# Two attentions in a row: an order of instructions planned by a list scheduler, queries in natural order, second scores over 128 rows, and a shared product for two tails

## The chip, the core and the metric

One NeuronCore of a Trainium2 chip runs the whole program. Its engines work side by side, each through its own instructions in order: TensorE (PE) multiplies matrices into PSUM, eight banks of 512 fp32 columns; VectorE (DVE) and ScalarE (ACT) read PSUM and write SBUF; GpSimd (POOL) works on SBUF alone; SyncE (SP) issues DMAs. Engines wait for each other by semaphores. The metric is the device time in microseconds.

## What is computed

For 8 batches and 8 heads of 576 positions and 64 columns, a first attention keeps only weights near the maximum; its heads side by side are the input x of a second, causal one with four experts, of which each position uses two. The reference in short, the sums and the gates' working left out:

```python
scores = scale * np.matmul(q, k.transpose(0, 1, 3, 2))
thresh = np.max(scores, axis=-1, keepdims=True) - tau
scores = np.where(scores >= thresh, scores, -1000000000.0)
attn = np.exp(scores - np.max(scores, axis=-1, keepdims=True))
x = (attn / sum) @ v                      # heads side by side: B, S, 512
...
for e in range(E):
    q, k, v = x @ wq[e], x @ wk[e], x @ wv[e]
    a = causal_softmax(scale * (q @ k.T))
    out += gate_e * (a @ v @ wo[e])       # gates: softmax of the 2 largest of x @ w_gate
```

## The kernel before

**Tiles.** A pair is two heads of one batch: 32 pairs. A pair has four score tiles of 128 queries by 576 keys for each head, and a fifth in which the 64 left-over queries of both heads stand as 128 rows, the *tail* (order of tiles: `TS = (4, 0, 1, 2, 3)`, 4 being the tail). fp32 operands are split into a rounded part (hi) and a rest (lo), and a product is hi·hi + hi·lo + lo·hi. DMAs spread k as `kt` and q as `qt` over 128 rows, so that two matmuls do for three terms (line 283). A loaded query tile holds every fourth position, since a partition takes four neighbouring rows of q at once; q and k are copied whole, and q scaled, before PE transposes them (`prep`, lines 256 to 310).

**First stage.** For a score tile: matmuls into one of two double banks `s`; VectorE takes the maximum (350) and the threshold `thr`, one instruction for each head (352); ACT the exponential (355); VectorE masks and sums (357); POOL normalizes (365); PE transposes `pp` (tm, tt), ACT or VectorE copies the results to `pt`, `ptt`; PE multiplies them by v in groups of tiles; the result is split into x.

**Second stage**, once for a batch, for two pairs of experts (`ep`): projections (pj), values (v) and gates; scores `s<-q,q` with 64-row operands, the two experts in the two halves of PE's rows, three terms each, then a mask; maximum, exponential, scaling on POOL; transposes (t), value products, and an output product of six 512-wide matmuls for each of five query tiles, the fifth of 64 rows. For the last batch the projections over two of the four pairs are made ahead and added later (`CUT`).

**Order.** PE's order is written out: each matmul follows the last by an explicit dependency, and a counter `pe[1]` adds up estimated PE time. Each of 160 first-stage steps has a share of 5.7 us; pieces of the second stage are put in when the counter passes a due time set at the piece before, transposes (T2) for instance so long after the scores:

```python
AFTER_S2, AFTER_V, AFTER_T2, AFTER_AV2 = 7000, 8500, 1800, 2000
...
        T2.append((pe[1] + AFTER_S2, b, t, ep))
```

The other engines are ordered by priorities (`PR`). The prediction names lines by the numbers of the listing.

Of the kernel before, what the change touches and what calls it, by code (L numbers as in the profile page):

```python
# [53 lines left out]
}  # L54
PPB = 4
P2B = 3
PTB = 9
PTTB = 4
VB = 3
E_PTT = "A"  # L60
# [3 lines left out]
def kernel(  # L64
# [13 lines left out]
    nc = tc.nc  # L78
    B, H, S, D = q.shape
    E = wq.shape[0]  # L80
    DM = H * D
    P = 128
    R = 4
    SM = R * P
    ST = S - SM
    HS = S // 2
    NPAIR = H // 2
    NC = DM // P
    EP = E // 2
    NV = E * D + E  # L90
    SCALE = 1.0 / math.sqrt(D)

    const = ctx.enter_context(tc.tile_pool(name="const", bufs=1))
    one = ctx.enter_context(tc.tile_pool(name="one", bufs=1))
    two = ctx.enter_context(tc.tile_pool(name="two", bufs=2))
    small = ctx.enter_context(tc.tile_pool(name="small", bufs=4))
    ps_s = ctx.enter_context(tc.tile_pool(name="ps_s", bufs=2, space=PSUM))
    ps_g = ctx.enter_context(tc.tile_pool(name="ps_g", bufs=4, space=PSUM))

    now = [0, 0]  # L100

    def pr(what):

        now[1] += 20
        tc.cur_priority = 20000000 + int((now[0] + PR.get(what, 0.0)) * 1000000) + now[1]

    def gbank(name, dt=F32):
        return ps_g.tile([P, 512], dt, tag="g", name=name)


    ident = const.tile([P, P], F32, name="ident")
    make_identity(nc, ident)
    ident_b = const.tile([P, P], BF16, name="ident_b")
    nc.gpsimd.tensor_scalar(ident_b, ident, 1.0, 0.0, op0=ALU.mult, op1=ALU.add)
    mask = const.tile([P, P], BF16, name="mask")
    nc.gpsimd.memset(mask, 0.0)
    nc.gpsimd.affine_select(out=mask, in_=mask, compare_op=ALU.is_ge, fill=NEG, base=0,
                            pattern=[[-1, P]], channel_multiplier=1)
    mask2 = const.tile([P, ST], BF16, name="mask2")
    nc.gpsimd.memset(mask2, 0.0)  # L120
    for j in range(2):
        nc.gpsimd.affine_select(out=mask2[j * ST:(j + 1) * ST], in_=mask2[j * ST:(j + 1) * ST],
                                compare_op=ALU.is_ge, fill=NEG, base=0,
                                pattern=[[-1, ST]], channel_multiplier=1)
    tie = const.tile([P, E, E], F32, name="tie")
    nc.gpsimd.memset(tie, 1.0)
    nc.gpsimd.affine_select(out=tie, in_=tie, compare_op=ALU.is_gt, fill=0.0, base=0,
                            pattern=[[1, E], [-1, E]], channel_multiplier=0)


    def rounded(dst, src, scale=1.0):
        nc.gpsimd.tensor_scalar(dst, src, scale, 0.0, op0=ALU.mult, op1=ALU.add)

    def rest(dst, src, hi):
        nc.gpsimd.tensor_tensor(dst, src, hi.bitcast(F32), op=ALU.subtract)

    def copy(e, dst, src):
        if e == "A":
            nc.scalar.activation(dst, src, AF.Copy)  # L139
        elif e == "D":  # L140
            nc.vector.tensor_copy(dst, src)
        elif e == "X":
            nc.any.tensor_copy(dst, src)  # L143
        else:
            rounded(dst, src)


    NOSYNC = mybir.DependencyInfo(mybir.DependencyClass.NoSync, mybir.DependencyReason.DATA)
    pe = [None, 0.0, None]

    def queued(r, x, ns):
        if pe[0] is not None:
            tc.add_manual_dep(r.ins, pe[0].name, NOSYNC, reason="order")
        shape = (x.shape[0], math.prod(x.shape[1:]))
        pe[0], pe[1], pe[2] = r.ins, pe[1] + ns + (190 if shape != pe[2] else 0), shape

    def matmul(out, x, y, **kw):
        w = math.prod(y.shape[1:])
        ns = 60 if x.dtype == BF16 else 0.81 * w if x.dtype == F32 else w / 2.4 + 11
        queued(nc.tensor.matmul(out, x, y, **kw), x, ns if x.shape[0] == P else ns / 2)  # L160

    def transpose(out, x):
        queued(nc.tensor.transpose(out, x, ident), x, 109)  # L163

    def minus(e, dst, a, b):
        (nc.vector if e == "D" else nc.gpsimd).tensor_tensor(dst, a, b, op=ALU.subtract)

    VS = {}  # L170
    qm = const.tile([P, 2, R + 1, D], F32, name="qm")
    km = const.tile([P, 2, R + 1, D], F32, name="km")
    for t in (qm, km):
        nc.vector.memset(t[ST:, :, R], 0.0)
    vtz = [const.tile([P, 2, D], F32, name=f"vtz{i}") for i in range(VB)]
    for t in vtz:
        nc.gpsimd.memset(t, 0.0)

    def load_pair(n):
        b, hp = divmod(n, NPAIR)  # L180
        hs = slice(2 * hp, 2 * hp + 2)
        vm = one.tile([P, 2, R, D], F32, tag="vm", name=f"vm_{n}", bufs=VB)
        pr("ld")
        def load(dst, src):
            r = nc.sync.dma_start(dst, src)
            if n in (1, 2):
                tc.add_manual_dep(r.ins, SPREAD[0].name, NOSYNC, reason="order")
        for t, x in ((km, k), (qm, q)):
            load(t[:, :, :R], x[b, hs, :SM, :].rearrange("h (p r) d -> p h r d", r=R))
            load(t[:ST, :, R], x[b, hs, SM:, :].rearrange("h s d -> s h d"))  # L190
        load(vm, v[b, hs, :SM, :].rearrange("h (p r) d -> p h r d", r=R))
        for j, rows in enumerate((slice(0, ST), slice(ST, P))):
            load(vtz[n % VB][rows, j], v[b, 2 * hp + j, SM:, :])
        VS[n] = (vm, vtz[n % VB])


    wqh = const.tile([P, NC, E * D], F32R, name="wqh")
    wql = const.tile([P, NC, E * D], F32R, name="wql")
    wkh = const.tile([P, NC, E * D], F32R, name="wkh")
    wkl = const.tile([P, NC, E * D], F32R, name="wkl")  # L200
    wvh = const.tile([P, NC, NV], F32R, name="wvh")
    wvl = const.tile([P, NC, NV], F32R, name="wvl")
    woh = const.tile([P, EP, DM], F32R, name="woh")
    wol = const.tile([P, EP, DM], F32R, name="wol")

    def load_weights(c, after):

        sl = slice(c * P, (c + 1) * P)
        begin = lambda t: nc.gpsimd.tensor_scalar(t, after, 1.0, 0.0, op0=ALU.mult, op1=ALU.add)
        pr("w")  # L210
        for w, wh, wl, sc in ((wq, wqh, wql, SCALE), (wk, wkh, wkl, 1.0), (wv, wvh, wvl, 1.0)):
            t = two.tile([P, E, D], F32, tag="st", name=f"wst{c}", bufs=PFB)
            begin(t[:, 0, :1])
            nc.sync.dma_start(t, w[:, sl, :].rearrange("e p d -> p e d"))
            tf = t.rearrange("p e d -> p (e d)")
            if sc != 1.0:
                rounded(tf, tf, sc)
            copy(E_W, wh[:, c, :E * D], tf)
            minus(E_W2, wl[:, c, :E * D], tf, wh[:, c, :E * D].bitcast(F32))
        g = small.tile([P, E], F32, tag="wgst", name=f"wgst{c}")  # L220
        begin(g[:, :1])
        nc.sync.dma_start(g, w_gate[sl, :])
        rounded(wvh[:, c, E * D:], g)
        rest(wvl[:, c, E * D:], g, wvh[:, c, E * D:])
        if c < EP:
            t = two.tile([P, DM], F32, tag="st", name=f"wost{c}", bufs=PFB)
# [626 lines left out]
```

## Time and profile before

| | |
|---|---|
| median of 3 runs | 1035.54 us (1034.78 to 1036.07) |
| span of the profiled execution | 1030.0 us |
| DMA | 96.11 MB; queue q1 34.5% of 16 engines |
| SP: waits of loads (line 185) for PE | 242.4 us |
| POOL: waits for VectorE's sums (line 365) | 321.5 us |

A group's row in the profile gives line, engine, operation, output and inputs, shape, count, then busy us, mean ns of one, and the idle time ahead of it with what ended it. A timeline row gives start and length in us first. The waits give who waited for whom: us in total, times, longest. Times of matmuls overlap: each runs to when its result is out.

### The profile page before, as it was taken

Reading aid. Unit: us, or ns where it says so; the run is one execution under the profiler, and the core shown is the slowest. Engines: PE = TensorE matmul, PEld = TensorE weight load, DVE = VectorE, ACT = ScalarE, POOL = GpSimd, SP = SyncE. Lnnn points to the kernel's source line nnn. Section 1 sums busy time; section 2 is a strip of 40 time slices with the busy share of each in tenths; the row PEclk is TensorE's granted clock in tenths of the full one; section 3 lists DMA queues with packets and bytes.
Section 4 is the critical chain, followed back from the end, with each engine's and each line's share of the span. In section 5 each row is a group of like instructions: output and inputs, shape, how many; then the busy total and the mean of one; then the engine's idle time right before and its main releaser. Section 6 shows DMA issues by size and latency. Waiting matters only on the chain.

```text
span 1030.0 us, 26586 instructions
## 1 busy us (share of the span) xinstructions
PE 952.2 (92%) x9520; PEld 853.2 (83%) x9520; DVE 824.8 (80%) x2380; ACT 649.8 (63%) x1558; POOL 408.5 (40%) x700
## 2 busy tenths in 40 slices
PE   3877999999999999999999999989999999999997
PEld 3777988789987898788987898878998789888975
DVE  3888788887888878878789878887788887888564
ACT  3676666766666656665667656676566665766544
POOL 2565425533344334443245332453334433433122
PEclk9899999999999999999999999999999999999999
DMA  6555423344223434324333342334422353311101
GB/s 158 144 148 147 123 64 81 94 127 120 76 58 89 132 102 103 81 49 134 91 102 102 79 127 62 89 100 128 122 60 57 96 142 102 80 45 30 43 1 46
DMA packets 83890, 96.11 MB, mean 93 GB/s; under 512 B 29744, under 2 KB 54320, under 8 KB 83760
## 3 DMA queue, kind: packets, MB, share of 16 engines
q1 hardware_dynamic: 83296, 93.83, 34.5%
q8 instruction: 76, 1.25, 0.5%
q10 hardware_dynamic: 464, 0.59, 0.2%
q14 instruction: 54, 0.44, 0.1%
HBM read 30.42 MB, written 9.44 MB: 39 GB/s over the span
## 4 chain that ended last, share of the span: by engine, by line
PE 68%; DVE 14%; ACT 10%; issue 4%; POOL 2%; DMA 2%; SPq 0%; DVEq 0%; ACTq 0%; POOLq 0%
PE av L160 18%; PE s L160 17%; PE tm L163 7%; PE pj L160 7%; PE o L160 6%; PE v L160 5%; PE t L163 4%; DVE pp L357 4%; ACT p L576 4%; ACT pp L355 2%; PE qkT L163 2%; DVE nm L574 2%; DVE nmx L350 2%; DVE x L440 1%; ACT pt L139 1%
## 5 line engine op out<-in xcount | busy, mean ns | idle before, releaser
L365 POOL TENSOR_SCALAR pp<-pp,ss 128x576 f32<-128x576 f32 x288 | 212.8, 750 | 404.4 <-DVE ss L371 321.5
L357 DVE SCALAR_TENSOR_TENSOR pp<-s,thr,pp 128x576 f32<-128x576 f32 x288 | 234.2, 814 | 69.2 <-ACT pp L355 61.9
L355 ACT ACTIVATE pp<-s,nmx 128x576 f32<-128x576 f32 x288 | 214.6, 746 | 73.4 <-DVE nmx L350 72.2
L350 DVE TENSOR_REDUCE nmx<-s 128x1 f32<-128x576 f32 x288 | 215.9, 752 | 35.1 <-PE s L160 34.0
L160 PE MATMUL s<-kt,qt 128*128 128x288 f32 x1024 | 198.2, 317 | 24.2 <-DVE pp L357 10.4
L160 PEld LDWEIGHTS s<-kt,qt 128*128 128x128 f32 x1024 | 150.6, 194 | 35.5 <-issue 16.0
L163 PE MATMUL tm<-ident,pp 128*128 128x128 f32 x1152 | 163.2, 277 | 1.1 <-POOL pp L365 0.3
L160 PE MATMUL av<-pt,vm 128*64 128x128 f32 (+1 forms) x2560 | 155.9, 265 | 0.0
L143 ACT COPY pt<-tm 128x512 f32<-128x512 f32 x193 | 110.7, 589 | 59.7 <-PE tm L163 57.6
L163 PEld LDWEIGHTS tm<-ident,pp 128*128 128x128 f32 x1152 | 136.0, 143 | 8.0 <-POOL pp L365 2.7
L160 PEld LDWEIGHTS av<-pt,vm 128*64 128x64 f32 x2560 | 130.6, 137 | 10.6 <-issue 6.5
L576 ACT ACTIVATE p<-s,nm 128x384 f32<-128x384 f32 (+3 forms) x144 | 78.7, 550 | 64.0 <-DVE nm L574 61.2
L590 POOL TENSOR_SCALAR p<-p,sm,gw 128x512 f32<-128x512 f32 (+3 forms) x128 | 77.2, 611 | 82.3 <-ACT pt L143 37.0
L139 ACT ACTIVATE x<-av 128x256 fp32r<-128x256 f32 (+1 forms) x96 | 48.3, 503 | 75.7 <-PE av L160 52.7
L574 DVE TENSOR_REDUCE nm<-s 128x1 f32<-128x384 f32 (+3 forms) x144 | 70.4, 512 | 23.4 <-PE s L160 19.9
L163 PE MATMUL t<-ident,p 128*128 128x128 f32 x384 | 61.5, 285 | 21.1 <-DVE ss L370 8.9
L163 PEld LDWEIGHTS t<-ident,p 128*128 128x128 f32 x384 | 42.2, 143 | 33.9 <-POOL p L590 14.3
L139 ACT ACTIVATE pt<-t 128x512 f32<-128x512 f32 (+2 forms) x112 | 58.0, 541 | 16.1 <-PE t L163 14.7
L440 DVE TENSOR_TENSOR x<-av,x 128x256 fp32r<-128x256 f32 (+1 forms) x96 | 47.3, 493 | 24.9 <-ACT x L139 22.3
L160 PE MATMUL v<-wvh,x 128*128 128x260 f32 x320 | 64.5, 287 | 0.0
L160 PE MATMUL av<-ptt,vtz 128*64 128x128 f32 (+1 forms) x640 | 59.1, 262 | 0.0
L160 PE MATMUL av<-pt,v 128*64 128x128 f32 (+1 forms) x896 | 55.8, 262 | 2.9 <-ACT p L576 2.4
(132 smaller groups left out, 1796.9 us busy)
## 6 DMA issues: line engine op xcount, KB each, us to landing
kt<-hl SPq DMA_DIRECT2D x252, 144.0 KB, 2.7
qt<-hl SPq DMA_DIRECT2D x128, 128.0 KB, 2.5
km<-in_k_dram SPq DMA_DIRECT2D x32, 256.0 KB, 3.0
qm<-in_q_dram SPq DMA_DIRECT2D x32, 256.0 KB, 3.2
vm<-in_v_dram SPq DMA_DIRECT2D x32, 256.0 KB, 2.8
out_dram<-ob SPq DMA_DIRECT2D x32, 256.0 KB, 2.3
km<-in_k_dram SPq DMA_DIRECT2D x32, 32.0 KB, 2.6
qm<-in_q_dram SPq DMA_DIRECT2D x32, 32.0 KB, 2.8
```

The source lines that it names most:

```text
L139: nc.scalar.activation(dst, src, AF.Copy)
L143: nc.any.tensor_copy(dst, src)
L160: queued(nc.tensor.matmul(out, x, y, **kw), x, ns if x.shape[0] == P else ns / 2)
L163: queued(nc.tensor.transpose(out, x, ident), x, 109)
L350: nc.vector.tensor_reduce(nmx[:, js], sv, axis=AX.XY, op=ALU.max, negate=True)
L355: nc.scalar.activation(e, sv, AF.Exp, bias=nmx[:, js])
L357: nc.vector.scalar_tensor_tensor(e, sv, thr[:, js], e, op0=ALU.is_ge, op1=ALU.mult, accum_out=ss[:, js])
L365: nc.gpsimd.tensor_scalar(p, p, ss[:, h:h + 1], 0.0, op0=ALU.mult, op1=ALU.add)
L440: nc.vector.tensor_tensor(xl, gs, xh.bitcast(F32), op=ALU.subtract)
L574: nc.vector.tensor_reduce(nmx[:, j:j + 1], sv, axis=AX.X if t < R else AX.XY, op=ALU.max, negate=True)
L576: nc.scalar.activation(p2[:, j * SM:j * SM + w] if t < R else halves(p2[:, :S]), sv, AF.Exp, bias=nmx[:, j:j + 1], accum_out=sm[:, j:j + 1])
L590: nc.gpsimd.tensor_scalar(p, p, sm[:, j:j + 1], gg[:, j:j + 1], op0=ALU.mult, op1=ALU.mult)
```

## The change

All functions are written anew. `work()` makes a list of tasks with their inputs, buffers, engines, durations and priorities; `plan()` runs through simulated time and, whenever an engine is free, starts the task of lowest priority number that is ready and finds its buffers free; copies from PSUM go to VectorE or ACT, whichever is free first. The kernel then writes every engine's instructions in that order.

- q is loaded head by head in natural order (runs of 256 bytes), k as before; PE transposes the loaded tiles themselves. ACT and VectorE scale q while they split it; only the tail's q is scaled ahead.
- Pair 0's scores use 64-row halves of the split q and k, no spread copies.
- Both heads' thresholds are one instruction; stt of either then follows both maxima.
- Second scores: DMAs copy q (hi in both row halves) and k (hi, lo, in both) into `qq`, eight DMAs for each `ep`; two 128-row matmuls for each expert, then its mask. Tiles of up to 256 columns share a bank and a maximum.
- The tails of two neighbouring batches stand as 128 rows of `zt` and share one output product.
- No projections made ahead for the last batch. Tail first, then tiles 2, 3, 0, 1; value products in groups (4, 2, 3) and (0, 1).

```diff
-AFTER_S2, AFTER_V, AFTER_T2, AFTER_AV2 = 7000, 8500, 1800, 2000
+CROSS, SELF, DRAIN, SWITCH, BEGIN = 75.0, 36.0, 165.0, 120.0, 800.0
+def t_act(n):
+    return 172 + 0.84 * n, 110
...
+def plan(tasks):
...
+        for e in engines:
+            if at[e] > now + 1e-9 or not ready[e]:
+                continue
+            best = begin(e, now)
+            if best is None:
+                continue
...
+            occ, lat = t.times[e]
+            at[e], t.end = start + occ, start + lat
...
+    def load_q(self, n, j, e):
+        self.dma(self.qi[:, :, j], self.q[b, 2 * hp + j, :SM, :].rearrange("(r p) d -> p r d", r=R), e)
...
+    def s_thr(self, sm, js):
...
+        self.nc.vector.scalar_tensor_tensor(m[:, 4 + a:4 + b], m[:, a:b], -1.0, self.tau_p[:, a:b], op0=ALU.mult, op1=ALU.subtract)
...
+    def spread_q2(self, q2, qq, j, x):
+        self.dma(self.qq(qq)[HEADS[x], j].bitcast(F32), self.q2(q2)[HEADS[j], x, :SM].bitcast(F32))
+    def spread_k2(self, k2, qq, j, r):
+        self.dma(self.qq(qq)[HEADS[r], 2 + 2 * j:4 + 2 * j].bitcast(F32), self.q2(k2)[HEADS[j], :, :SM].bitcast(F32))
...
-            for i, (x, y) in enumerate(HHL):
-                for j in range(2):
...
-                    matmul(gg[j][:, :w], q2[sl, x, t * P:w], k2[sl, y, :w], start=(i == 0), stop=False)
+        for j in range(2):
...
+            for x in range(2):
+                self.mm(g[:, o:o + w], u[:, j, t * P:w], u[:, 2 + 2 * j + x, :w], x == 0, False)
+            self.mm(g[:, o + t * P:o + w], self.ident_b, self.mask, False, True)
...
+    def z_hi(self, z, b, t, ep, g, m):
+        o = 0 if t < R else (b % 2) * ST
+        self.copy("ACT", self.z(z)[:, 0, ep, o:o + m], self.bank(g)[:, :m])
...
+    with tc.manual_schedule():
+        em = Emit(ctx, tc, q, k, v, tau, w_gate, wq, wk, wv, wo, out)
+        for t in plan(work(em)):
+            t.fn()
```

PE at the start of the program, before (`s_0_4` is pair 0's tail, `s_0_0_0` the first head's tile 0 from the spread `kt` and `qt`):

```order
L163 MATMUL qkT_0_640_143<-ident_73,ki_119 128x128 x4
L163 MATMUL qkTt_0_150<-ident_73,qi_118 128x128
L163 MATMUL qkTt_0_150<-ident_73,ki_119 128x128
L163 MATMUL qkT_0_0_162<-ident_73,qi_118 128x128 x4
L160 MATMUL s_0_4_0_189<-hl_0_138,qd0_114 128x288 x6
L160 MATMUL s_0_0_0_212<-kt_0_140,qt_0_139 128x288 x4
```

and now (`qq0` holds pair 0's split q and k; `s0` and `s2` are the two heads' score banks):

```order
L758 MATMUL g7_3_137<-ident_71,ki_66 128x128 x4
L758 MATMUL g6_4_143<-ident_71,qit_67 128x128
L758 MATMUL g6_4_143<-ident_71,kit_68 128x128
L758 MATMUL g5_6_149<-ident_71,qi_65 128x128 x4
L761 MATMUL s0_7_164<-qq0_5_146 128x288
L761 MATMUL s2_8_166<-qq0_5_146 128x288
```

The first scores read the split tile itself, the two heads by turns, and the tail comes third.

PE at a second score tile of 512 columns, before (two experts, three terms, then the masks):

```order
L160 MATMUL s2_3_3_0_0_7698<-q2_3_0_1_7467,q2_3_0_0_7380 128x512
L160 MATMUL s2_3_3_0_1_7699<-q2_3_0_1_7467,q2_3_0_0_7380 128x512
L160 MATMUL s2_3_3_0_0_7698<-q2_3_0_1_7467,q2_3_0_0_7380 128x512
L160 MATMUL s2_3_3_0_1_7699<-q2_3_0_1_7467,q2_3_0_0_7380 128x512
L160 MATMUL s2_3_3_0_0_7698<-q2_3_0_1_7467,q2_3_0_0_7380 128x512
L160 MATMUL s2_3_3_0_1_7699<-q2_3_0_1_7467,q2_3_0_0_7380 128x512
```

and now (`qq0` the copies; `g5` and `g4` the two experts' banks):

```order
L761 MATMUL g5_1360_7523<-qq0_1297_7143 128x512 x2
L761 LDWEIGHTS ident_b_98
L761 MATMUL g5_1360_7523<-mask_100,ident_b_98 128x128
L761 MATMUL g4_1361_7527<-qq0_1297_7143 128x512 x2
L761 LDWEIGHTS ident_b_98
L761 MATMUL g4_1361_7527<-mask_100,ident_b_98 128x128
```

Four matmuls stand where six stood, and each expert's mask follows its own.

SP in the middle of the program, before:

```order
L185 DMA km_97<-in_k_dram 64x2x64
L283 DMA kt_14_5832<-hl_14_5830 64x576 x6
L283 DMA qt_14_5831<-hl_14_5830 64x512 x4
L185 DMA qm_96<-in_q_dram 128x2x256
L185 DMA qm_96<-in_q_dram 64x2x64
```

and now (`qq0<-q20` and `qq0<-k20` are the copies of the second scores, `out` a store):

```order
L764 DMA qt0_938_5199<-hl0_913_5049 64x512 x4
L764 DMA qi_65<-in_q_dram 128x4x64 x2
L764 DMA out_0_dram<-ob0_951_5259 128x512
L764 DMA vm1_86<-in_v_dram 128x2x256
L764 DMA vt1_90<-in_v_dram 64x64 x2
L764 DMA qq0_965_5337<-q20_953_5274 64x512 x4
L764 DMA out_0_dram<-ob0_972_5378 128x512
L764 DMA qq0_965_5337<-k20_967_5353 64x2x512 x4
L764 DMA ki_66<-in_k_dram 128x4x64 x2
```

Eight copies for each `ep` have joined the one queue, with a store between those of q and those of k.

More of the change, by code (lines that the diff above doesn't have):

```diff
@@ L1 @@
+import bisect
+import heapq
 import math
@@ L55, with __init__ @@
[L55 to L60, printed above, removed]
+B, H, S, D = 8, 8, 576, 64
+E = 4
+DM = H * D
+P = 128
+R = 4
+SM = R * P
+ST = S - SM
+HS = S // 2
+NPAIR = H // 2
+NC = DM // P
+EP = E // 2
+NV = E * D + E
+SCALE = 1.0 / math.sqrt(D)
+NPR = B * NPAIR
+HHL = ((0, 0), (0, 1), (1, 0))
+HEADS = [slice(j * D, (j + 1) * D) for j in range(2)]
+KO = SM + ST
+J1 = S + ST
+TS = (4, 2, 3, 0, 1)
+GROUPS = ((4, 2, 3), (0, 1))
+SLOTS = {
[3 rows of a table added]
+}
+class Buf:
+    def __init__(self, cls):
+        self.cls, self.left, self.slot, self.ap = cls, 0, None, None
@@ new lines, with __init__, behind @@
+class Task:
+    def __init__(self, times, fn, deps, pri, takes, uses, cols, ld, name, at):
+        self.times, self.fn, self.pri, self.cols, self.ld, self.name = times, fn, pri, cols, ld, name
+        self.engines = tuple(times)
+        self.move = 0.0
+        self.takes = takes
+        self.uses = list(dict.fromkeys([*takes, *uses]))
+        self.wait, self.after, self.ready, self.start, self.end, self.by = 0, [], at, None, None, None
+        for d in deps:
+            self.behind(d)
+        for b in self.uses:
+            b.left += 1
+    def behind(self, other):
+        other.after.append(self)
+        self.wait += 1
@@ L77 @@
 ):
[L78 to L113, printed above, removed]
@@ L125 @@
[L125 to L145, printed above, removed]
@@ L148 @@
[L148 to L194, printed above, removed]
@@ L197 @@
[L197 to L226, printed above, removed]
-            begin(t[:, :1])
-            nc.sync.dma_start(t, wo[2 * c:2 * c + 2].rearrange("e d f -> (e d) f"))
-            copy(E_W, woh[:, c], t)
-            minus(E_W2, wol[:, c], t, woh[:, c].bitcast(F32))
@@ L645, in output @@
-    def output(b, t):
-        m = P if t < R else ST
-        zh, zl = Z.pop((b, t))
-        pr("o")
-        o = gbank(f"o_{b}_{t}")
-        n = 0
-        for ep in range(EP):
-            for x, w in ((zh, woh), (zh, wol), (zl, woh)):
-                matmul(o, x[:, ep], w[:, ep], start=(n == 0), stop=(n == 5))
-                n += 1
-        pr("ob")
-        ob = two.tile([P, DM], F32, tag="st", name=f"ob_{b}_{t}", bufs=PFB)
-        copy(E_OB, ob[:m], o[:m])
-        nc.sync.dma_start(out[b, t * P:t * P + m, :], ob[:m])
@@ L716, in transpose_tile @@
-    def transpose_tile():
-        _, b, t, ep = T2.pop(0)
-        transp2(b, t, ep)
-        A2.append((pe[1] + AFTER_T2, b, t, ep))
-    def piece():
-        if due(O2):
-            output(*O2.pop(0)[1:])
-        elif transposable():
-            transpose_tile()
-        elif not project_some():
-            return False
-        return True
-    def fill(until):
-        while pe[1] < until and piece():
-            pass
-    def tiled():
-        for _ in range(2):
-            if due(A2):
-                value_tile()
-        if S2 and S2[0][2] < R and len(T2) < P2B:
-            score_tile()
@@ L807 @@
-    goal = since = pe[1]
-    while proj or S2 or T2 or A2 or O2:
-        if pe[1] > goal:
-            now[0] += 1
-            goal += STEP
-        if due(O2):
-            output(*O2.pop(0)[1:])
-        elif due(A2):
-            value_tile()
-        elif transposable():
-            transpose_tile()
-        elif S2 and len(T2) < (P2B if S2[0][1] < B - 1 else PPB) and pe[1] >= since:
-            score_tile()
-            since = pe[1] + BETWEEN_S2
-        elif not project_some():
-            pe[1] += 100
+    with tc.manual_schedule():
+        em = Emit(ctx, tc, q, k, v, tau, w_gate, wq, wk, wv, wo, out)
+        for t in plan(work(em)):
+            t.fn()
```

1389 lines of the change are left out of this document (880 added, 509 removed), and 11 rows, old and new, of tables (PR, SLOTS).

## Prediction

> **What bounds the kernel now.** I read the page's first part, then busy time by stretch, then the timeline for the rate at which TensorE starts matmuls, then the waits.
>
> ```profile
> span 1030.0 us, 26586 instructions
> PE 952.2 (92%) x9520; PEld 853.2 (83%) x9520; DVE 824.8 (80%) x2380; ACT 649.8 (63%) x1558; POOL 408.5 (40%) x700
> ```
>
> TensorE (PE) is busiest and VectorE (DVE) not far behind. A matmul's row includes the time its result takes to come out, so a pause shorter than that is hidden in the 92%. The rate of starts shows what PE really needs:
>
> ```profile
> 405.18 0.70 PE L160 MATMUL s<-kt,qt 128*128 128x288 f32 x4
> 405.72 1.03 PE L163 MATMUL tm<-ident,pp 128*128 128x128 f32 x8
> 406.59 0.30 PE L163 MATMUL tt<-ident,pp 128*128 128x128 f32 x1
> ...
> 982.53 0.28 PE L160 MATMUL v<-wvl,x 128*128 128x260 f32 x1
> 982.65 0.40 PE L160 MATMUL v<-wvh,x 128*128 128x260 f32 x2
> ...
> 719.06 0.39 PE L160 MATMUL o<-wol,zh 128*128 128x512 f32 x1
> 719.29 0.40 PE L160 MATMUL o<-woh,zl 128*128 128x512 f32 x1
> ...
> 974.32 1.04 PE L160 MATMUL av<-pt,vm 128*64 128x128 f32 x16
> ```
>
> Columns are start, length, engine, line, operation and count. Four 288-wide matmuls of about 0.30 us fill 0.70, so one starts every 0.133 us; transposes every (406.59-405.72)/8 = 0.109, 260-wide ones every 0.12, 512-wide ones every 0.23; the value products stand as two rows each and start a row every (1.04-0.27)/15 = 0.051, or 0.055 with the turns between groups. The program has 2,080 of 288, 480 of 260, 2,032 transposes, 240 of 512, 3,200 value rows of 128 columns and 960 of half that: 277 + 58 + 221 + 56 + 176 + 28 = 816 us. Second scores and their masks add 53 (below), and 198 changes between 128-wide and 64-wide outputs 18 (0.09 each). **PE work is about 887 us**; the rest of the span is pauses. Where they lie:
>
> ```profile
> core 0: us, PE busy (x) PEld busy (x) DVE busy (x) ACT busy (x) POOL busy (x), PEclk, DMA share, GB/s
> 0.00:107.00 107.00, 75.76 (x709) 68.76 (x709) 76.73 (x216) 63.77 (x129) 55.41 (x121) 0.94 0.59 151
> 107.00:936.40 829.40, 791.31 (x8045) 712.05 (x8044) 691.92 (x1997) 537.15 (x1295) 330.94 (x542) 1.00 0.36 93
> 936.40:975.60 39.20, 38.95 (x386) 35.53 (x386) 26.99 (x72) 22.11 (x54) 8.61 (x13) 1.00 0.09 31
> 975.60:1030.00 54.40, 46.22 (x386) 36.90 (x386) 29.17 (x96) 26.78 (x80) 13.50 (x24) 0.97 0.07 23
> ```
>
> The cuts are the first tail score of pair 4 (107.0), that of pair 31 (936.4) and the last first-stage value product (975.6). By the same count in the program's order PE works 61, 748, 38 and 41 us in them. So the pauses are 46, **82**, 1 and 13 us, the last with 4 us after the final matmul. The first stretch has no second-stage work to fill gaps; the second has, and still stands 10% of its time. PE's weight loads tell for whom:
>
> ```profile
> PEld s L160 <- issue: 26.1, 59, 3.3
> PEld t L163 <- POOL p L590: 14.3, 14, 2.1
> ...
> PEld t2t L163 <- ACT pt L139: 6.9, 7, 1.0
> PEld t L163 <- issue: 6.7, 22, 0.5
> ...
> PEld t L163 <- DVE x L440: 4.3, 7, 0.6
> PEld t L163 <- POOL qd L132: 4.1, 7, 0.6
> ```
>
> The five rows of t and t2t, 36 us, are one thing: PE has been put in front of a second-stage transpose before its probabilities are scaled. The rest are mostly score tiles (s) that wait for one of two score buffers, which VectorE must empty.
>
> **The change, part by part.** *Work of PE.* Eight tail products of the output become four: 24 matmuls of 512 fewer, 24 x 0.23 = -5.6 us. Second scores, before, at the widest tile:
>
> ```profile
> 627.34 0.96 PE L160 MATMUL s<-q,q 64*128 64x512 f32 x6
> 628.23 0.29 PE L160 MATMUL s<-mask,ident_b 128*128 128x128 bf16 x2
> ...
> 636.83 0.80 PE L160 MATMUL s<-q,q 64*128 64x384 f32 x6
> ...
> 660.12 0.81 PE L160 MATMUL s<-q,q 64*128 64x256 f32 x6
> ...
> 668.17 0.55 PE L160 MATMUL s<-q,q 64*128 64x128 f32 x6
> ```
>
> Six matmuls of 64 rows hold PE for 0.89 us, until the mask starts; the narrower ones, 0.07 off each row likewise, 0.73, 0.74 and 0.48: 2.84 for the four. After, each is four of 128 rows: 4 x 0.23 = 0.92, on the line through 0.133 and 0.23 then 0.71 and 0.48, and at 128 columns between that line and a transpose's 0.109, 0.25 to 0.44, say 0.32: 2.43. Times 16: -6.6 us. A pair of halves costs 0.30 at 512 columns, not 0.23, which is why two terms of 128 rows match three of 64. The masks, one by one now, may take 2 us more. The Trainium skill, TensorE: Matmul & The Clock Gate, Part 3 (The mechanism), states that matmuls on different row groups run side by side, a tile adding some 4 ns. By that, pairs would cost as much as one 128-row matmul, 3 against 4, and this edit would cost time rather than save it, 16 x (2.43/4) = 10 us more; the 512-wide row here doesn't agree, since three pairs took 0.89 and not 0.69.
>
> Pair 0's scores now use 64-row halves straight from the split q and k: four tiles of six pairs at about 0.235 (between 256 and 512 wide) against 32 starts of 0.133, +1.4. Fewer changes of output width: -0.5. **PE work 878 us.** The order puts 62, 730, 37 and 50 us of it in the four stretches: second-stage work moves to the end, because the last batch's projections are no longer half done ahead.
>
> *Start.* Three things go:
>
> ```profile
> 6.99 1.09 PE L163 MATMUL qkT<-ident,ki 128*128 128x128 f32 x4 [6.99 <-ACT ki L261]
> ...
> 17.60 1.30 PE L160 MATMUL s<-kt,qt 128*128 128x288 f32 x4 [5.42 <-DMA qt<-hl]
> ...
> 18.94 0.76 DVE L350 TENSOR_REDUCE nmx<-s 128x1 f32<-128x576 f32 x1 [3.94 <-PE s L160]
> ```
>
> The copy of k ahead of the transposes, the query side's copy, and the wait of 5.4 us for spread copies. Transposes can begin near 5.2, scores near 8.7 and VectorE's maxima near 10.3, about 8 us ahead of 18.94. VectorE then paces the batch (76.7 us busy of 107): without 16 threshold rows (3 us) it can run at most as fast as its work, about 82 us with copies it takes over, from 7 on. I take pair 4 at **97** instead of 107, bounds 92 and 104.
>
> *VectorE.*
>
> ```profile
> L352 DVE SCALAR_TENSOR_TENSOR thr<-nmx,tau_p 128x1 f32<-128x1 f32 x288 | 54.5, 190 | 2.1
> ...
> L143 DVE COPY pt<-tm 128x512 f32<-128x512 f32 x59 | 40.0, 679 | 1.6 <-PE tm L163 1.6
> ...
> L139 ACT ACTIVATE ptt<-tt 128x128 f32<-128x128 f32 (+1 forms) x192 | 51.0, 265 | 1.7 <-PE tt L163 0.4
> ...
> L141 DVE COPY ob<-o 128x512 f32<-128x512 f32 (+1 forms) x40 | 27.2, 680 | 5.2 <-PE o L160 5.2
> ```
>
> The threshold of both heads in one instruction: 128 fewer x 0.19 = -24.3. Outputs copied by ACT: 23 x 0.68 = -15.6. Smaller mergers (32 maxima, 32 x-remainders, the partial sums): by estimate -16. Against that the planner gives VectorE 57 more pt copies (x 0.68 = +38.7) and 81 ptt copies (about +21). Net +4: VectorE keeps 829 us of work while PE's span shrinks, so it becomes tighter. ACT gives up these copies and POOL the full copies of q and k; neither is on the path.
>
> *The order.* The old code put second-stage pieces by fixed PE times after their scores; the new one simulates all engines and puts a task on PE when its inputs and a PSUM bank are there. Its constants agree with the rows above (0.109 a transpose, 0.133 a 288-wide matmul), so I let the 36 us of t and t2t go. What is late next is the score buffer. Between a tile's scores and its first transpose stands a median of 11.5 us of PE work instead of 9.3, but between uses of a score buffer 4.7 instead of 5.1. I leave 32 of the remaining 46 us; bounds 0, and 80 if the share of pauses stays.
>
> *Copies of the second scores.* 128 more DMAs; SyncE issues 845 instead of 664.
>
> ```profile
> 407.86 1.22 SPq L185 DMA_DIRECT2D qm<-in_q_dram  x2
> ```
> ```profile
> kt<-hl SPq DMA_DIRECT2D x252, 144.0 KB, 2.7
> ```
> ```profile
> L475 DVE TENSOR_TENSOR q<-pj,q 128x288 fp32r<-128x288 f32 x56 | 25.5, 455 | 11.8 <-ACT q L139 11.6
> ```
>
> After the last projection come two evictions (0.9), four issues of 0.61 and a landing of about 2.7: 6 us. The order has 7.2 to 18.9 us of PE work there, 9.2 in most second halves, so I cost them at nothing; that work is the cover. If gone, each of 16 groups would stand up to 6 us, 96 in all. Queued behind those four issues are output stores and the next pair's loads, which have 13 us or more of PE work ahead of their use.
>
> *End.* 50 us of PE work instead of 41, with 11 us of pauses (9 now, plus the wait for the last x before a projection): 61, then 4.
>
> **Sum.** 97 + (730+32) + 39 + 61 + 4 = 963 against 1030. The median of before is 5.5 over its profiled span: 968.5, say **968**.
>
> **Rivals.** (1) VectorE becomes the bound. Its best stretch now:
>
> ```profile
> 500.00:600.00 100.00, 94.46 (x995) 83.41 (x994) 85.12 (x251) 66.40 (x161) 40.53 (x66) 1.00 0.34 90
> ```
>
> At 85% busy the 696 us of its steady work take 818 instead of 762: 1025. For it: two buffers and a threshold that now waits for both heads' maxima. Against: a 100-us stretch at 85% is no ceiling, and the planner hands it copies only when it is free. (2) The order doesn't do what it says: the 10% of pauses stay, 730/0.90 = 811, and the time is 1017. (3) Slower: SyncE. One in-order queue carries loads, copies and stores; a store that waits for its output stands between the q and the k copies of a group. If copies land more than 13.4 us after their projection, the wait is 4.2 us past the usual 9.2, and 16 of them are 67 us: 1035. From there it is slower; at the full 6 us, 1064. Against: SyncE's 845 x 0.61 = 515 us is about half the time. (4) Pairs of 64 rows are as good as one matmul of 128: then 10 us are lost where I count 6.6 as won, and the time is 985; the rows above speak against it. It is the rule of the Trainium skill's page named above.
>
> **How the numbers follow.** Forecast 0.62; VectorE 0.12; pauses stay 0.12; pairs 0.02; SyncE or an order that stalls likewise 0.10; the two cancel 0.02. All but the last two are faster: faster 0.88, within 0.2% (what a measurement of this kernel can tell) 0.02, slower 0.10. The range reaches from no steady pause and pair 4 at 93 (93+730+39+61+4+5.5 = 932) to VectorE's 1025.
>
> **What would show it.** Right: PE starts near 5 us; no 5-us wait for a copy of q; pair 4's tail score near 97; fewer than 10 us of waits of second transposes; VectorE at 87 to 91% in the middle; the last value product near 900. Wrong: PE idle with DMA or SyncE as releaser at second scores; VectorE over 95% busy with PE behind it; an end longer than 70 us.

## The result and the profile after

The changed kernel takes **969.83 us** (median of 4 runs, 969.72 to 969.98) against 1035.16 us (1034.38 to 1036.07) in the same session: a ratio of 0.9369, 95% interval 0.9356 to 0.9383. The forecast was 968, its range 932 to 1025.

The first part of its page:

```profile
span 968.0 us, 26132 instructions
PE 929.4 (96%) x9384; PEld 852.2 (88%) x9384; DVE 818.2 (85%) x2278; ACT 601.8 (62%) x1406; POOL 366.5 (38%) x635
```

And its busy time by stretch, with the same cuts as before (tail score of pair 4, of pair 31, last first-stage value product):

```profile
core 0: us, PE busy (x) PEld busy (x) DVE busy (x) ACT busy (x) POOL busy (x), PEclk, DMA share, GB/s
0.00:105.70 105.70, 80.14 (x727) 69.54 (x727) 83.61 (x216) 56.29 (x110) 48.06 (x98) 0.92 0.55 133
105.70:871.60 765.90, 758.26 (x7769) 702.45 (x7770) 675.98 (x1895) 499.32 (x1162) 293.98 (x497) 1.00 0.54 129
871.60:910.60 39.00, 38.56 (x459) 34.76 (x460) 30.20 (x84) 23.75 (x59) 12.18 (x18) 1.00 0.17 42
910.60:968.00 57.40, 52.48 (x436) 45.41 (x432) 28.39 (x84) 22.48 (x76) 12.33 (x22) 1.00 0.36 88
```

| stretch, us | before | forecast | measured |
|---|---|---|---|
| to pair 4's tail | 107.0 | 97 | 105.7 |
| to pair 31's tail | 829.4 | 762 | 765.9 |
| to the last value product | 39.2 | 39 | 39.0 |
| to the end | 54.4 | 65 | 57.4 |
| time over the span | 5.5 | 5.5 | 1.8 |

The second stretch lost 63.5 us, the whole span 62. What TensorE waited for there shows in its weight loads. Of before, the four longest rows of that stretch; its rows of score tiles (s) add to 23 us and those of t and t2t to 35:

```profile
PEld t L163 <- POOL p L590: 10.1, 7, 1.4
PEld L160 <- issue: 8.6, 28, 0.4
PEld s L160 <- issue: 7.2, 42, 0.2
PEld t2t L163 <- ACT pt L139: 6.9, 7, 1.0
```

Of the changed kernel (g is any single bank, its second transposes among them; s is a score buffer), the longest of the same stretch, then its longest of s, whose rows add to 5.5 us there:

```profile
PEld L761 <- issue: 11.1, 52, 0.3
PEld g L758 <- issue: 5.8, 15, 1.1
PEld g L761 <- issue: 5.2, 31, 0.2
...
PEld s L761 <- DVE pp L890: 2.2, 11, 0.3
```

All rows of the stretch add to 100 us before and 49 now. The second transposes by themselves waited 41 us in the whole span before (the last figures of a row are the weight loader's idle time ahead of them, in all and by what ended it):

```profile
L163 PEld LDWEIGHTS t<-ident,p 128*128 128x128 f32 x384 | 42.2, 143 | 33.9 <-POOL p L590 14.3 <-issue 6.7 <-DVE x L440 4.3
L163 PEld LDWEIGHTS t2t<-ident,p 128*128 128x128 f32 x16 | 2.2, 140 | 6.9 <-ACT pt L139 6.9
```

and 8 now:

```profile
L758 PEld LDWEIGHTS g<-ident,p 128*128 128x128 f32 x400 | 45.8, 140 | 7.9 <-issue 4.3 <-POOL p L1121 1.7 <-POOL qd L751 1.0
```

So both kinds of pause went, those at second transposes and those at score tiles. Which of them mattered, and whether VectorE stood behind it, the pauses can't say; the experiments say part of it. Each ratio below is against the kernel before in the same session, and 0.001 is 1.0 us.

### The profile page after: what moved, and what is told of

The parts are those of the page before. It is cut to its first block, busy times and chain, and to the rows that moved or that the text cites. A ratio compares the mean times of both kernels' runs of the same rounds, so it can differ in the third digit from the quotient of the medians.

```text
span 968.0 us, 26132 instructions
## 1 busy us (share of the span) xinstructions
PE 929.4 (96%) x9384; PEld 852.2 (88%) x9384; DVE 818.2 (85%) x2278; ACT 601.8 (62%) x1406; POOL 366.5 (38%) x635
## 4 chain that ended last, share of the span: by engine, by line
PE 69%; DVE 17%; ACT 2%; POOL 1%; issue 1%; DMA 0%; DVEq 0%; ACTq 0%; SPq 0%; POOLq 0%
PE g L761 40%; PE g L758 17%; PE s L761 13%; DVE sm L873 4%; DVE pp L890 4%; DVE sm L1093 2%; DVE pt L749 1%; DVE sm L895 1%; ACT pt L747 1%; ACT p L1101 1%; POOL p L1121 1%; DVE sm L899 0%; DVE sm L878 0%; DVE x L755 0%; DVE hl L755 0%
## 5 line engine op out<-in xcount | busy, mean ns | idle before, releaser
L903 POOL TENSOR_SCALAR pp<-pp,sm 128x576 f32<-128x576 f32 x288 | 213.3, 752 | 328.2 <-DVE sm L899 240.9
L885 ACT ACTIVATE pp<-s,sm 128x576 f32<-128x576 f32 x288 | 212.1, 742 | 76.8 <-DVE sm L873 68.8
L873 DVE TENSOR_REDUCE sm<-s 128x1 f32<-128x576 f32 x304 | 226.5, 750 | 27.8 <-PE s L761 24.3
L890 DVE SCALAR_TENSOR_TENSOR pp<-s,sm,pp 128x576 f32<-128x576 f32 x288 | 227.9, 812 | 7.9 <-ACT pp L885 2.0
L747 ACT ACTIVATE pt<-g 128x512 f32<-128x512 f32 (+2 forms) x284 | 159.6, 580 | 64.9 <-PE g L758 62.5
L758 PE MATMUL g<-ident,pp 128*128 128x128 f32 x1312 | 188.8, 278 | 9.6 <-POOL pp L903 6.6
L758 PEld LDWEIGHTS g<-ident,pp 128*128 128x128 f32 x1312 | 153.9, 143 | 16.7 <-POOL pp L903 10.4
L761 PE MATMUL g<-pt,vm 128*64 128x128 f32 (+1 forms) x2560 | 157.1, 265 | 1.2 <-DVE pt L749 1.2
L761 PEld LDWEIGHTS g<-pt,vm 128*64 128x64 f32 x2560 | 133.8, 138 | 8.1 <-issue 4.3
L761 PE MATMUL g<-x,wh 128*128 128x288 f32 x512 | 107.0, 302 | 0.7 <-DVE q L755 0.2
```

Of the source, the lines that this page charges most:

```text
L747: self.nc.scalar.activation(dst, src, AF.Copy)
L758: self.nc.tensor.transpose(out, x, self.ident)
L761: self.nc.tensor.matmul(out, x, y, start=first, stop=last)
L873: self.nc.vector.tensor_reduce(self.small(sm)[:, j:j + 1], self.dbank(s)[:, :, :HS], axis=AX.XY, op=ALU.max, negate=True)
L885: self.nc.scalar.activation(e, self.dbank(s)[:, :, :HS], AF.Exp, bias=self.small(sm)[:, j:j + 1])
L890: self.nc.vector.scalar_tensor_tensor(e, self.dbank(s)[:, :, :HS], m[:, 4 + j:5 + j], e, op0=ALU.is_ge, op1=ALU.mult, accum_out=m[:, 2 + j ...
```

## Experiments

**Second transposes later, in the kernel before.**

```diff
-AFTER_S2, AFTER_V, AFTER_T2, AFTER_AV2 = 7000, 8500, 1800, 2000
+AFTER_S2, AFTER_V, AFTER_T2, AFTER_AV2 = 9500, 11000, 1800, 2000
```

> The kernel before, with the second stage's transposes set 2.5 us of TensorE time later behind their scores or values (7.0 and 8.5 us become 9.5 and 11.0; the changed order has a median of 11.5). Nothing else is changed. Main theory (in the kernel before TensorE stood in front of second transposes whose probabilities weren't scaled, 36 us, and the new order's gain in the steady stretch is largely this): 1005 to 1022 us against 1035, the rows of t and t2t under 12 us. Rival (the pause only moves to score tiles that wait for VectorE): 1028 to 1045, with the rows of t and t2t gone and those of s grown by as much.

1035.38 us; ratio 1.0000 (0.9984 to 1.0017): nothing. Its longest rows of the second stretch, with those of s and t:

```profile
PEld s L160 <- issue: 12.3, 31, 2.5
PEld s L160 <- DVE pp L357: 7.8, 17, 1.1
PEld s L160 <- ACT p L576: 5.4, 8, 1.3
...
PEld t L163 <- issue: 3.2, 11, 1.0
PEld t2t L163 <- ACT p L576: 2.6, 4, 0.8
```

The rows of t and t2t fell from 35 to 12 us, those of s rose from 23 to 37. The windows show the rest:

```profile
107.50:917.10 809.60, 771.33 (x7864) 700.82 (x7863) 682.81 (x1971) 520.30 (x1252) 322.95 (x529) 1.00 0.37 95
917.10:1033.10 116.00, 105.33 (x952) 87.78 (x950) 64.98 (x199) 60.43 (x172) 29.48 (x50) 0.97 0.06 22
```

The second stretch is 19.8 us shorter, but 181 matmuls, by count some 17 us, have moved to the end, which is 22.4 longer. The rival holds in the time, though the rows of s grew by less than those of t and t2t lost: taken away alone, this wait comes back at score tiles and in a longer end, and nothing is won.

**One threshold instruction, in the kernel before.**

```diff
-            nc.vector.scalar_tensor_tensor(thr[:, js], nmx[:, js], -1.0, tau_p, op0=ALU.mult, op1=ALU.subtract)
...
+            if j == nj - 1:
+                nc.vector.scalar_tensor_tensor(thr[:, :nj], nmx[:, :nj], -1.0, tau_p[:, :nj], op0=ALU.mult, op1=ALU.subtract)
+                for h in range(nj):
+                    nc.vector.scalar_tensor_tensor(e[h], sps[h][:, :, :HS], thr[:, h:h + 1], e[h], op0=ALU.is_ge, op1=ALU.mult, ...)
```

> The kernel before, with the threshold of both heads in one VectorE instruction: 128 fewer, 24 us less of VectorE's 825, and the first head's comparison now waits for the second head's maximum too. Nothing else is changed. Theory A (VectorE isn't the bound, and the fixed order decides): 1028 to 1037 us, no more than 7 of the 24 come through. Theory B (VectorE's work decides how soon score buffers come free): 1010 to 1020 us.

1055.49 us; ratio 1.0205 (1.0171 to 1.0240): slower by 21 us, which neither theory had. The row of score tiles that wait for the comparison, 5.8 us in this stretch before:

```profile
PEld s L160 <- DVE pp L360: 37.9, 40, 1.6
```

The first head's comparison now stands behind the second head's maximum, so the first of two score buffers comes free later. (The profiled execution was the slowest of its six, 1063.6 us.) This edit alone is a loss in the old order; that it helps in the new one, no run shows.

**Two threshold instructions, in the changed kernel's own order.**

```diff
-        self.nc.vector.scalar_tensor_tensor(m[:, 4 + a:4 + b], m[:, a:b], -1.0, self.tau_p[:, a:b], op0=ALU.mult, op1=ALU.subtract)
+        for a in js:
+            self.nc.vector.scalar_tensor_tensor(m[:, 4 + a:5 + a], m[:, a:a + 1], -1.0, self.tau_p[:, a:a + 1], op0=ALU.mult, op1=ALU.subtract)
```

> The changed kernel in exactly its order, but where the threshold of both heads is one VectorE instruction, two stand behind each other. 128 more instructions of about 0.19 us: 24 us more for VectorE (818 of 968 us), with no other task moved. Theory A (TensorE's work and the order bound the steady stretch; VectorE at 88% has room): 971 to 978 us, a third of the 24 or less comes through. Theory B (VectorE bounds it): 988 to 994 us, nearly all of the 24.

969.85 us; ratio 0.9365 (0.9338 to 0.9392): no change. But the load was far smaller than I meant. Of this run, from VectorE's timeline:

```profile
404.10 0.22 DVE L878 SCALAR_TENSOR_TENSOR sm<-sm,tau_p 128x1 f32<-128x1 f32 x2
```

Of the changed kernel:

```profile
405.46 0.16 DVE L878 SCALAR_TENSOR_TENSOR sm<-sm,tau_p 128x2 f32<-128x2 f32 x1
```

The second instruction adds 0.06 us, not 0.19, so 128 of them add 8; VectorE's busy time rose by only 3.5, to 821.7. So some 4 to 8 us of added VectorE work cost nothing that can be told here. As a test of theory B this is weak.

**Each head's threshold its own task, planned anew.**

```diff
-ONETHR = True
+ONETHR = False
```

> The changed kernel, but the threshold of each head is an instruction of its own again (256 instead of 128, as in the kernel before). It adds 128 x 0.19 = 24.3 us to VectorE's 818, and nothing to TensorE. Theory A (TensorE's work and the order bound the time; VectorE at 88% has room): 968 to 978 us, at most a third of the 24 comes through. Theory B (VectorE bounds the steady stretch, and the gain came from relieving it): its added work comes through in full, 990 to 996 us, with VectorE near 88% again in a longer stretch.

983.62 us; ratio 0.9522 (0.9505 to 0.9539), 16 us more. The next run shows why this can't be read as the instruction's price.

**A null change of the plan.**

```diff
-    "stt": -1.49, "sum": 1.76, "nrm": -2.56, "tm": 1.22, ...
+    "stt": -1.49, "sum": 1.76, "nrm": -2.56, "tm": 1.27, ...
```

> The changed kernel with one of the planner's priorities moved by 0.05 of a pair (the second transposes'), which reorders tasks here and there and changes no work. It tells how far the time depends on the accident of one plan. If the gain is that of the method: 965 to 975 us. If this order is a lucky one among many: 980 or more.

984.07 us; ratio 0.9512 (0.9499 to 0.9526): 15 us more by one priority. The edit moves `tm`, which is the priority of the first stage's transposes; that of the second transposes is `t2`, and it stayed. As a null change it serves all the same. The method holds most of its gain, this order about 15 us more than this one neighbour. The planner gave VectorE more copies here, 831.5 us busy against 818.2, and the weight loads of s behind the comparison wait 9.8 us in the span instead of 3.7. With the two further down, tails apart and three score buffers, four plans made anew with true times stand 16, 15 and 6 us above the changed kernel and 2 below it. So only runs in the same order price a single edit.

**Some VectorE copies twice, in the same order.**

```diff
-...K.copy(e, K.t(pt, [P, SM]), K.bank(g))...
+...K.copy_pt(e, K.t(pt, [P, SM]), K.bank(g))...
...
+    def copy_pt(self, e, dst, src):
+        self.copy(e, dst, src)
+        if e == "DVE":
+            self.npt = getattr(self, "npt", 0) + 1
+            if self.npt % 2 == 0:
+                self.copy(e, dst, src)
```

> The changed kernel in exactly its order, but every second one of the 128x512 copies of first-stage probabilities that VectorE makes is made twice, one behind the other: some 40 more copies, which start 0.61 us apart (a row of 0.687 less the 0.07 by which such rows overlap), 24 us more for VectorE, and so much later for what stands behind them. Theory A (VectorE has room; TensorE's work bounds the steady stretch): 968 to 978 us, a third or less comes through. Theory B (VectorE bounds it): 988 to 995 us.

992.95 us; ratio 0.9592 (0.9563 to 0.9621), 23 us more: theory B. From its page:

```profile
span 991.7 us, 26186 instructions
PE 936.6 (94%) x9384; PEld 854.0 (86%) x9384; DVE 843.5 (85%) x2317; ACT 602.0 (61%) x1406; POOL 365.1 (37%) x635
```

VectorE's 25 us came through nearly whole, while its busy share stayed at 85%: 5.5 us in the first stretch (111.2 instead of 105.7) and 17 in the steady one (782.9 instead of 765.9). That share had looked like room and, for these copies, was none. At this rate the 13 us more of VectorE in the null change would be worth 12 of its 15.

**A quarter of the maxima over half a row, in the same order.**

```diff
+        self.nm = getattr(self, "nm", 0) + 1
+        h = 2 if self.nm % 4 else 1
-        ...tensor_reduce(self.small(sm)[:, j:j + 1], self.dbank(s)[:, :, :HS], axis=AX.XY, op=ALU.max, negate=True)
+        ...tensor_reduce(self.small(sm)[:, j:j + 1], self.dbank(s)[:, :h, :HS], axis=AX.XY, op=ALU.max, negate=True)
```

> The mirror of the run with copies made twice: the changed kernel in exactly its order, but every fourth maximum of first-stage scores (76 of 304) reads only the first 288 of its 576 columns, so that maximum, threshold and exponential of those tiles come from half a row. That is 0.3 us less each (the rows for 576 and 288 columns differ by as much), 23 us less for VectorE, and TensorE's work unchanged. Theory A (TensorE and VectorE hold each other up in a fixed order: added VectorE time came through in full, but TensorE's 730 us of work in 766 us leave little to win): 957 to 966 us. Theory B (VectorE alone bounds the steady stretch): 945 to 952 us, as much as was taken away.

964.02 us; ratio 0.9319 (0.9296 to 0.9341): 5 us less by the medians, 9.5 by the profiled spans (the profiled execution was the fastest of its five), for 24 us of VectorE (794.3 busy). Theory A. The pages give shares of the chain that ended last. The changed kernel:

```profile
PE 69%; DVE 17%; ACT 2%; POOL 1%; issue 1%; DMA 0%; DVEq 0%; ACTq 0%; SPq 0%; POOLq 0%
```

with the copies twice:

```profile
PE 61%; DVE 24%; ACT 2%; issue 2%; DMA 1%; POOL 1%; DVEq 0%; SPq 0%; POOLq 0%; ACTq 0%
```

and with the shorter maxima:

```profile
PE 83%; DVE 10%; ACT 2%; POOL 1%; DMA 1%; issue 1%; ACTq 0%; DVEq 0%; SPq 0%; POOLq 0%
```

What is taken away from VectorE hands most of its part to TensorE. The 24% of the added copies say less: two other runs in the same order, the one with two thresholds and the one with masks together below, have 16% and 22% without them. The two edits also lie at different places, copies behind the first stage's transposes and maxima ahead of its exponentials, so whether the sign or the place makes the difference isn't separated.

**A planner that is told wrong times.**

```diff
+        t = {e: (u[0] * 0.6, u[1] * 0.6) if e in ("DVE", "POOL") else u for e, u in t.items()}
```

> The changed kernel, whose planner is told that VectorE's and POOL's tasks take 0.6 of their time. The tasks are the same and TensorE's work is 878 us as before; only the order and the share of copies between VectorE and ACT differ. Main theory (the 46 us that the pauses of the steady stretch lost come from an order made with the engines' real times): pauses return, above all at score tiles, the steady stretch takes 785 to 815 us and the whole 985 to 1020. Rival (they come from what the tasks are, such as a threshold for both heads and the shared products, and any order that runs tasks when the planner deems them ready will do): 965 to 980 us.

1142.31 us; ratio 1.1036 (1.1001 to 1.1072): far past my range, and slower than the kernel before. Its page:

```profile
PE 994.9 (87%) x9384; PEld 865.0 (76%) x9384; DVE 916.7 (80%) x2485; ACT 517.6 (45%) x1199; POOL 364.6 (32%) x635
...
DVE 52%; PE 31%; issue 5%; POOL 5%; ACT 3%; DMA 2%; SPq 0%; DVEq 0%; ACTq 0%; POOLq 0%
```

The planner loaded 98 us more on VectorE (916.7 against 818.2), and VectorE now holds half the chain. If that came through as in the run with copies twice (23 of 25), some 82 of the 172 us are left for waits of the order; the run doesn't separate the two. The steady stretch takes 909.7 us, and the longest row of waits in it is a second transpose in front of probabilities that aren't scaled, the very wait that was to go:

```profile
PEld g L759 <- POOL p L1122: 36.1, 45, 2.6
```

TensorE's tasks are the same: a plan made with wrong durations gives back the whole gain and more. So the plan, order and share of copies together, is needed for the gain.

**Tails apart.**

```diff
-        if b % 2 == 0:
-            ZT[b // 2], ZTD[b // 2] = Buf("zt"), []
-        z[R] = ZT[b // 2]
+        z[R] = Buf("zt")
...
```

> The changed kernel, but each batch's tail has an output product, an eviction and a store of its own again (64 rows of output instead of 128 for two batches). It adds 24 matmuls of 512 columns (24 x 0.23 = 5.6 us of TensorE) and 4 evictions. Theory A (TensorE's work counts in full): 975 us, 5 to 7 more than the changed kernel's 969.8. Rival (pauses soak up work that TensorE is given, or the shared tail costs something by holding back the first batch's output): 966 to 971.

974.37 us; ratio 0.9425 (0.9412 to 0.9438), 5.8 us more, as theory A has it. But this run was planned anew too, and a null change of the plan moved the time by 15 us, so the agreement may be chance.

**Masks of the two wide tiles together, in the same order.**

```diff
-            self.mm(g[:, o + t * P:o + w], self.ident_b, self.mask, False, True)
+            if nar:
+                self.mm(g[:, o + t * P:o + w], self.ident_b, self.mask, False, True)
+        for j in range(0 if nar else 2):
+            self.mm(self.bank(gs[j])[:, t * P:w], self.ident_b, self.mask, False, True)
```

> The changed kernel, but the two tiles of 512 and 384 columns of each expert pair issue their two bf16 masks one after the other, behind both experts' products, instead of a mask behind each expert's product. The same matmuls otherwise, in the same order of tasks. Theory: the matmul that follows a bf16 mask starts some 0.1 us late, so the tile of 512 takes about 1.10 instead of 1.21 us and that of 384 0.78 instead of 0.88 on TensorE; 16 groups x 0.2 = 3 us, 966 to 968 us. Rival (the switch costs nothing, and the tiles are long for another reason, such as weight loads of 128 rows): 969.8, the tiles' lengths unchanged.

971.18 us (967.92 to 973.13); ratio 0.9393 (0.9374 to 0.9412): no gain that can be told. The tile did get shorter. A tile of 512 columns in the changed kernel, from TensorE's timeline:

```profile
145.32 0.73 PE L761 MATMUL g<-qq 128*128 128x512 f32 x2
145.89 0.23 PE L761 MATMUL g<-mask,ident_b 128*128 128x128 bf16 x1
145.93 0.71 PE L761 MATMUL g<-qq 128*128 128x512 f32 x2
146.48 0.23 PE L761 MATMUL g<-mask,ident_b 128*128 128x128 bf16 x1
146.53 0.65 PE L761 MATMUL s<-kt,qt 128*128 128x288 f32 x3
```

and with the masks together:

```profile
144.52 1.20 PE L761 MATMUL g<-qq 128*128 128x512 f32 x4
145.55 0.28 PE L761 MATMUL g<-mask,ident_b 128*128 128x128 bf16 x2
145.65 0.78 PE L761 MATMUL s<-kt,qt 128*128 128x288 f32 x4
```

1.21 us against 1.13, until the next matmul starts, and nearly as much less at 384 columns: sixteen times the two is 2.3 us, about what the mechanism says. The total doesn't show it. A gain of 2.3 us would be a ratio 0.0022 lower, and the ratio is 0.0024 higher, further off than the two intervals allow. So what these tiles save did not reach the end, and why isn't shown.

**Warm first pairs, in the same order.**

```diff
-        for c in range(R):
+        self.nt = getattr(self, "nt", 0) + 1
+        for c in [*range(R)] * (3 if self.nt <= 32 else 1):
```

> The changed kernel in exactly its order, but each group of four first-stage transposes is done three times over into the same bank for the first 32 groups (some four head pairs): 32 x 8 x 0.109 = 28 us of added TensorE work in the stretch to pair 4's tail score, which has 44 us of pauses and four spells of half the clock, 17 us together. Theory 1 (the spells follow TensorE's pauses and hold the stretch up): the spells go, and the stretch takes 105 us or less in spite of the work; 960 to 970 us. Theory 2 (TensorE waits there for scaled probabilities behind VectorE, and the spells cost little or come from something else): the spells stay or go, and the stretch grows by 5 to 28 us; 975 to 998 us.

987.29 us; ratio 0.9537 (0.9507 to 0.9568): theory 2. The clock, from windows of the changed kernel:

```profile
23.50:26.90 3.40, 3.37 (x19) 2.69 (x20) 2.03 (x6) 0.79 (x3) 0.75 (x1) 0.50 0.71 174
50.80:57.60 6.80, 6.16 (x30) 5.36 (x31) 5.51 (x13) 3.70 (x6) 3.31 (x5) 0.50 0.47 105
```

and of this run:

```profile
23.50:26.90 3.40, 3.02 (x27) 2.79 (x26) 1.86 (x5) 1.88 (x4) 1.47 (x2) 1.00 0.68 175
50.80:57.60 6.80, 5.05 (x51) 4.66 (x48) 4.89 (x13) 2.08 (x4) 1.48 (x2) 1.00 0.73 180
```

All spells but one, of 3.4 us, are gone, yet pair 4's tail comes at 124.3 us instead of 105.7: 18.6 us for 28 of added work. So the spells follow TensorE's pauses: filled with work, they go. What they cost isn't separated. In 17 us at half the clock TensorE does the work of 8.5, so the spells can have cost up to 8.5 us; with these given back, 28 of added work leave 19.5, close to the 18.6. Pauses that took up a third of the added work would give the same.

**Three score buffers early, planned anew.**

```diff
-EARLY = 0.0
+EARLY = 100000.0
...
+        self.banks = self.psum.tile([P, 8, 512], F32, tag="banks", bufs=1, name="banks")
...
+            if buf.cls in "sg":
+                buf.ap = self.banks[:, buf.slot] if buf.cls == "g" else self.banks[:, buf.slot:buf.slot + 2]
```

> The changed kernel, planned with three score buffers and two single banks instead of two and four up to 100 us of the planner's time. Theory 1 (the first stretch, 105.7 us where 97 was predicted, waits for the two score buffers): pair 4's tail score at 92 to 101 us and the whole at 956 to 966. Theory 2 (it waits for VectorE's chain of maximum, comparison and inverse and for POOL's scaling behind it, which a third buffer doesn't shorten): pair 4's tail at 104 to 109 us, the whole at 967 to 980.

967.95 us; ratio 0.9359 (0.9326 to 0.9391): the whole can't be told from the changed kernel, which is in theory 2's range, and no run that computes everything beats it by more than the intervals. But pair 4's tail starts at 100.0 us, within theory 1:

```profile
99.98 0.92 PE L765 MATMUL banks<-hl,qd 128*128 128x288 f32 x3
```

The other three plans made anew with true times have it at 104.7, 105.4 and 107.9. But the earlier tail is mostly another order of tasks. The window up to it:

```profile
0.00:100.00 100.00, 75.34 (x656) 65.64 (x657) 79.62 (x210) 52.35 (x103) 43.99 (x93) 0.92 0.60 141
```

71 matmuls fewer stand ahead of the tail than in the changed kernel (656 against 727), most of them value products, by the prediction's prices some 4 us, and VectorE has 4 us less to do. TensorE's waits for the comparison are 8.9 us in the changed kernel's window and 8.8 in this one. Up to pair 31's tail, where the matmuls are level again, this run is 3.5 us ahead (868.1 against 871.6), less than a null change of the plan can make. So the run doesn't show that the score buffers cost the first stretch its time.

## Why the prediction was right

The mechanism was right, its reasons only in part.

- **The steady stretch, term 730 + 32: size right.** 762 was forecast and 765.9 measured.

  The 730 was too low. Second scores, forecast at -6.6 and +2 for the masks, saved nothing: undisturbed tiles, until the next matmul starts, took 0.99, 0.82, 0.82 and 0.58 us before (medians at 512, 384, 256 and 128 columns) and 1.21, 0.89, 0.64 and 0.62 now. Their sum is 0.15 more, times 16 is +2.4 instead of -4.6.

  The reading "a pair of halves costs 0.30 at 512 columns, not 0.23" was wrong. It spread 0.89 evenly over three pairs; by their starts, in the kernel before,

```profile
627.34 0.50 PE L160 MATMUL s<-q,q 64*128 64x512 f32 x2
627.67 0.40 PE L160 MATMUL s<-q,q 64*128 64x512 f32 x2
627.91 0.39 PE L160 MATMUL s<-q,q 64*128 64x512 f32 x2
```

  the first pair holds TensorE 0.33 us, the second 0.24 and the third, ahead of the bf16 mask at 628.23, 0.32. Four products of 128 rows, in the run with the masks together, start likewise:

```profile
144.52 0.50 PE L761 MATMUL g<-qq 128*128 128x512 f32 x1
144.85 0.39 PE L761 MATMUL g<-qq 128*128 128x512 f32 x1
```

  0.33 for the first, then (145.55-144.85)/3 = 0.23 each. So between the edges a pair of halves costs what one product of 128 rows costs, and four stand for three at 512 columns; only at 256 is the new tile shorter. That is the rule of rival 4, which I thought the rows spoke against and gave 0.02. Its price, 16.6 us more than I counted, came to 7, in part since a tile of 256 gained 0.18.

  So TensorE's work is about 885 us instead of 878, 2 less than before. With 6 of these 7 us in the steady stretch its pauses are 766 - 736 = 30 us, where I had 32. Nearly the whole gain is pauses: by count 82 before, where the other 12 us by which this stretch shrank are work that moved to the start and the end.
- **"I let the 36 us of t and t2t go": the rows went, the reason was short.** With later transposes alone, in the old order, score tiles took over the pause. Of the five rows that I called one thing only the largest, 14.3, names the scaled probabilities; the others name copies, x and a split, or nothing. Later transposes shortened them all the same. The gain came where both kinds went: in the new order the rows of s fell too. Which part did that, the priorities, the pooled banks, the earlier work or the lighter ACT and POOL (48 and 42 us less busy), wasn't separated; that the planner needs durations near the true ones is shown (1142 us without).
- **VectorE: the share was right (88%; 87 to 91 forecast), its meaning wrong.** I took "a 100-us stretch at 85% is no ceiling" for room. The copies made twice came through with 23 of 25 us. Rival 1's end, 1025, was still wrong: VectorE's work fits the 766 us. It is a co-bound: more copies cost nearly in full, shorter maxima bring a fifth to two fifths, and second thresholds cost nothing that can be told. Its work was 818 us, not 829: with 8 instead of 24 for the thresholds my sum would be 845, so the copies and mergers were mis-sized too, by some 27 the other way.
- **The threshold, -24.3: mis-sized.** A row's mean overlaps its neighbour. The start interval gives 0.06 x 128 = 8 us, and in this order putting it back cost nothing.
- **Shared tails, -5.6: not contradicted**; 5.8 was measured, under a new plan.
- **Copies at nothing: right.** No row of TensorE waits for a copy of second scores; the only DMA it waits for is the first load:

```profile
PE g L758 <- DMA ki<-in_k_dram: 5.8, 1, 5.8
```

  though those of k landed later than my 2.7 us:

```profile
qq<-k SPq DMA_DIRECT2D x64, 256.0 KB, 4.2
qq<-q SPq DMA_DIRECT2D x64, 128.0 KB, 2.4
```

- **The start, 97: wrong.** Transposes began at 5.8 and scores at 9.3, 0.6 late each, and VectorE's first maximum at 11.9, 1.6 late. VectorE's 83.6 us of work there were near the 82 that I had. But I left it 97 - 7 - 82 = 8 us of pauses behind its start, and it had 105.7 - 7 - 83.6 = 15. What these pauses wait for isn't shown; the run with a third score buffer doesn't settle it.
- **The end, 65: 8 too long**; of its 11 us of pauses some 3 came.
- **The offset, 5.5: wrong.** Time over span was 1.7 us in this profiled run and 1.7 to 2.1 in all of the experiments, so most of the 5.5 was probably the profiled execution of before being quicker than its median.

The misses of +9, +4, -8 and -4 cancelled. 969.8 is closer to 968 than the terms deserve, and that is luck; the neighbouring plan's 984 would have missed by 16.

## What to carry to other kernels

When a pause at one place is removed, ask who pauses next and test it on the old order: here 23 us less of one wait won nothing. A busy share of 85% was not room in this fixed order; price it by adding load in the same order, and by taking it away: here the two differed two- to fourfold, though at different places. Before pricing an edit under a planner, measure a null change of the plan (15 us here), and take the cost of overlapping instructions from start to start, one by one: a mean over a tile put its edges into the price of a pair.

## What the runs showed of the hardware

- A bf16 mask between two fp32r products costs more than its own 0.04 us: two products of 512 columns behind it take 0.55 us, where the last two of four in a row take 2 x 0.23. The weight loader also stands 0.21 us ahead of 52 loads of the mask's weights in the steady stretch, 11.1 us; with the masks together these waits were 32 instead of 64 in the span.
- TensorE's granted clock halves in spells of 3.4 or 6.8 us in the first 100 us of the changed kernel and nowhere in its steady stretch; with more transposes there all but one spell, of 3.4 us, vanished. The Trainium skill, TensorE: Matmul & The Clock Gate, Part 1 (What's actually happening), states that the clock is gated to half unless activity in a window of about 3.4 us is high, and the spells agree. What they cost wasn't separated.
- Two 64-row fp32r matmuls in the two halves of PE's rows cost together what one of 128 rows does: at 512 columns a pair between two others held TensorE 0.24 us, a 128-row product 0.23.
- VectorE starts a second tiny instruction 0.06 us after the first, though each row is 0.16 to 0.19 long.
